# Two attention layers: reciprocal sums applied in the output projection, a ninth P tile, and maxima turned by VectorE

## The chip, the cores and the metric

The kernel runs on one core of a Trainium2 chip. TensorE (PE) multiplies, ACT evaluates exponentials and copies, VectorE (DVE) reduces and does arithmetic between tiles, GpSimd (POOL) adds tiles and issues some DMAs, SyncE (SP) issues most DMAs. Each engine runs its own queue of instructions in order and waits on semaphores for the others. The metric is the device time of one execution in microseconds; lower is better.

## The reference

Two layers of the same kind follow each other. Each is attention over 2048 tokens of width 1024 with 32 heads of width 32, then a routed feed-forward block for the eight best tokens:

```
h   = layernorm(x)
q, k, v = split(h @ wqkv)                  # 32 heads of 32
p   = softmax(q k^T * 32**-0.5)            # 2048 x 2048 per head
x   = x + (p v) @ wo                       # output projection
h   = layernorm(x);  r = h @ w_r           # router score per token
top = 8 tokens with the largest r
y   = (silu(h[top] @ w_gate) * (h[top] @ w_up)) @ w_down
x   = x + h;  x[top] += y * sigmoid(r[top])   # residual of the layernormed rows
```

What matters here: softmax needs the maximum of each row before the exponential, and the sum of the exponentials after it. The kernel multiplies unnormalised exponentials with v and divides by the sum later.

## The kernel before

A layer has three stages: layernorm and the projection to q, k, v; attention; the output projection with the router. The feed-forward block of layer 0 runs beside the start of layer 1.

**Attention** is cut into 32 units per layer. A unit is a group of four heads (g, eight of them) and a quarter of the queries (qc, 512 of them). A unit has 16 steps, one for each 128 keys; step s belongs to unit u = s // 16 and key tile kt = s % 16. In a step TensorE computes the scores of four heads (`scores`, L457), ACT exponentiates them into a tile P (128 × 2048, L767), and TensorE multiplies the P tile of the step before with v (`pv_step`, L685). Besides, TensorE computes plain scores 22 steps ahead (`pre_mm`, L442), and VectorE reduces them to negated maxima (L450), for a later unit. When a unit's maxima are complete, `nm_combine` (L463) takes the minimum over four parts, and `nm_row` (L466 to L475) turns the 128 × 16 result: TensorE transposes it, ACT copies it, SP stores it to DRAM and loads it into one row of the q tile, where it takes part in the product of the scores.

The sum of the exponentials of a unit runs over its 16 P tiles. `MERGED` (L34) names pairs of tiles that a DMA of GpSimd's queue adds in place (`merge`, L700). `ADDED` (L35) names the additions into an accumulator on GpSimd (`acc_add`, L697) as pairs (step, tile). `DIRECT` (L36) names tiles that TensorE sums itself. At step 20 (`SUM_AT`), `sum_mm` (L707) multiplies the direct tiles and the accumulator with ones, four groups in all. `sum_out` copies the result (L714) and stores it, `sum_load` loads it narrow, `recip` inverts it (L724) and stores it, `r_load` loads it broadcast over 32 rows per head, and `norm` lets GpSimd multiply the unit's result with it (L737) and stores the product to `oT` in DRAM. `unit_events` gives the step, the place within the step and the order of each of these. There are eight buffers for P (`PB`); a tile's buffer comes free when its product with v and its merge, addition or sum are done. In the last unit of a layer VectorE does the additions (twelve), and its sum stays in PSUM: VectorE inverts and applies it (L831, L832) after the first weights of the next stage are ready.

**The output projection** (L842 to L878) takes 16 tiles of 128 tokens. `load_o(t)` loads all heads of a tile of tokens from `oT` into `oraw` (two buffers), `split_o(t)` makes two parts of it for the product: ACT rounds (L813), VectorE takes the remainder (L814). The products with `woh` and `wol`, the two parts of the weights, follow (L848, L849, L852). In the loop for tile t VectorE adds the residual (L854), then `split_o(t + 2)`, then the layernorm's statistics (L118, L120), GpSimd works on the statistics (L122 to L862), and SP stores them (`mrd`). After that SP's queue has `load_o(t + 4)`, the load of the residual of tile t + 2, the store of tile t and one load of feed-forward weights.

All orders are those of the program text: each engine executes its instructions in the order in which the loops issue them, and tiles wait for their buffers.

## Time and profile before

| What | Value |
|---|---|
| time, median of 3 runs | 4825.82 us (4814.48 to 4838.82) |
| time of the profiled execution | 4831.82 us |
| its span, first to last instruction | 4829.9 us |
| mean granted TensorE clock | 0.981 |
| busy: PE, DVE, POOL, ACT | 97%, 66%, 63%, 50% |
| exponentials of layer 0, first to last | 613.0 to 2133.6 us |
| exponentials of layer 1, first to last | 3002.5 to 4528.4 us |

A row of a group gives line, engine, operation, output and inputs, the count, the busy time and the mean of one in ns, then the idle time of the engine before these instructions and what ended it. A row of a timeline gives the start and length in us, engine, line, operation, and in brackets the idle time before it with what ended it. SPq are DMAs issued by SP; their length is that of the issue, not of the transfer. A row of stretches gives the stretch, its length, and the busy time of PE, PEld (weight loads), DVE, ACT and POOL, then the granted clock, the share of the DMA engines and GB/s.

### The profile page before, as it was taken

Reading aid. Unit: us, or ns where it says so; the run is one execution under the profiler, and the core shown is the slowest. Engines: PE = TensorE matmul, PEld = TensorE weight load, DVE = VectorE, ACT = ScalarE, POOL = GpSimd, SP = SyncE. Lnnn points to the kernel's source line nnn. Section 1 sums busy time; section 2 is a strip of 40 time slices with the busy share of each in tenths; the row PEclk is TensorE's granted clock in tenths of the full one; section 3 lists DMA queues with packets and bytes.
Section 4 is the critical chain, followed back from the end, with each engine's and each line's share of the span. In section 5 each row is a group of like instructions: output and inputs, shape, how many; then the busy total and the mean of one; then the engine's idle time right before and its main releaser. Section 6 shows DMA issues by size and latency. Waiting matters only on the chain.

```text
span 4829.9 us, 75205 instructions
## 1 busy us (share of the span) xinstructions
PE 4662.7 (97%) x30014; PEld 2737.4 (57%) x30014; DVE 3177.4 (66%) x4919; ACT 2437.1 (50%) x2612; POOL 3023.1 (63%) x1249
## 2 busy tenths in 40 slices
PE   8999999999999999999799999999999999999996
PEld 6887654544445544448577777445444454454572
DVE  3221478888888888875522225888888888888653
ACT  2222266666666666651122222666666666666400
POOL 4443367787778787854433332777777777787551
PEclk9999999999999999999999999999999999999997
DMA  6656477777777777737679564777767677777488
GB/s 196 184 175 176 140 158 156 170 163 152 172 149 166 164 157 161 174 86 235 211 246 270 182 178 133 161 154 164 164 148 170 152 156 169 157 164 166 106 223 288
DMA packets 360815, 832.61 MB, mean 172 GB/s; under 512 B 55000, under 2 KB 187096, under 8 KB 310528
## 3 DMA queue, kind: packets, MB, share of 16 engines
q1 hardware_dynamic: 313296, 494.18, 34.6%
q0 software_dynamic: 47168, 333.63, 34.3%
q8 instruction: 235, 3.85, 0.3%
q14 instruction: 116, 0.95, 0.1%
HBM read 383.47 MB, written 119.14 MB: 104 GB/s over the span
## 4 chain that ended last, share of the span: by engine, by line
PE 79%; DMA 12%; DVE 2%; issue 2%; POOL 2%; SPq 1%; ACT 1%; POOLq 0%; ACTq 0%; DVEq 0%
PE pv L685 18%; PE pre L457 16%; PE st L442 13%; PE st L553 7%; PE st L555 7%; PE st L554 7%; PE st L707 4%; DMA out_dram<-x,pi 3%; DMA P<-P 2%; POOL acc L697 2%; DMA nmx<-nmr 1%; PE pre L852 1%; PE pre L849 1%; PE pre L848 1%; DMA q<-nmx 1%
## 5 line engine op out<-in xcount | busy, mean ns | idle before, releaser
L450 DVE TENSOR_REDUCE nm<-st 128x1 f32<-128x512 f32 x3920 | 2438.9, 684 | 472.7 <-PE st L442 459.5
L767 ACT ACTIVATE P<-pre 128x1024 f32<-128x1024 f32 x2048 | 1985.2, 1022 | 781.0 <-PE pre L457 573.4
L697 POOL TENSOR_TENSOR acc<-acc,P 128x2048 f32<-128x2048 f32 x372 | 1737.6, 4671 | 58.1 <-DMA P<-P 35.2
L457 PE MATMUL pre<-q,ks 64*128 64x512 f32 (+1 forms) x8192 | 1170.6, 399 | 26.9 <-ACT P L767 15.4
L685 PE MATMUL pv<-P,v 128*32 128x512 f32 x8192 | 1101.7, 610 | 2.6 <-DMA v<-vd 2.6
L442 PEld LDWEIGHTS st<-ks,q 64*128 64x128 f32 x3920 | 553.2, 185 | 882.6 <-DVE nm L450 732.9
L442 PE MATMUL st<-ks,q 64*128 64x512 f32 x3920 | 998.6, 469 | 7.3 <-DVE nm L450 5.8
L457 PEld LDWEIGHTS pre<-q,ks 64*128 64x128 f32 (+1 forms) x8192 | 790.5, 188 | 213.9 <-ACT P L767 75.6
L499 POOL TENSOR_TENSOR wl<-wraw,wh 128x2048 fp32r<-128x2048 f32 (+1 forms) x97 | 441.9, 4556 | 677.4 <-ACT wh L498 664.8
L553 PE MATMUL st<-xh,wh 128*128 128x512 f32 x1536 | 616.7, 401 | 2.2 <-ACT xh L525 2.2
L555 PE MATMUL st<-xl,wh 128*128 128x512 f32 x1536 | 602.0, 392 | 0.6 <-DVE xl L526 0.5
L554 PE MATMUL st<-xh,wl 128*128 128x512 f32 x1536 | 601.0, 391 | 0.0
L700 POOL DMA_DIRECT2D P<-P x310 | 272.0, 887 | 298.5 <-PE st L442 258.7
L697 POOL TENSOR_TENSOR acc<-P 128x2048 f32<-128x2048 f32 x62 | 283.9, 4579 | 259.7 <-DMA P<-P 237.6
L569 DVE TENSOR_TENSOR lo<-st,hi 128x512 fp32r<-128x512 f32 x128 | 88.3, 690 | 433.5 <-ACT hi L568 433.5
L568 ACT CAST hi<-st 128x512 fp32r<-128x512 f32 x128 | 75.3, 588 | 558.6 <-PE st L555 553.2
L553 PEld LDWEIGHTS st<-xh,wh 128*128 128x128 f32 x1536 | 290.0, 189 | 104.3 <-issue 30.5
L555 PEld LDWEIGHTS st<-xl,wh 128*128 128x128 f32 x1536 | 289.8, 189 | 64.6 <-DVE xl L526 1.7
L554 PEld LDWEIGHTS st<-xh,wl 128*128 128x128 f32 x1536 | 290.3, 189 | 56.3
L685 PEld LDWEIGHTS pv<-P,v 128*32 128x32 f32 x8192 | 162.2, 108 | 268.5 <-issue 262.9
L535 DVE COPY vn<-st 128x512 f32<-128x512 f32 x64 | 44.3, 692 | 318.5 <-PE st L533 318.5
L848 PE MATMUL pre<-woh,oh 128*128 128x512 f32 x512 | 201.8, 394 | 11.8 <-DVE woh L827 5.7
(163 smaller groups left out, 2649.4 us busy)
## 6 DMA issues: line engine op xcount, KB each, us to landing
P<-P POOLq DMA_DIRECT2D x310, 1024.0 KB, 8.2
wraw<-in_A_wqkv_dram SPq DMA_DIRECT2D x96, 1024.0 KB
q<-qh SPq DMA_DIRECT2D x256, 128.0 KB
ks<-kh SPq DMA_DIRECT2D x128, 256.0 KB
fw<-in_B_w_down_dram SPq DMA_DIRECT2D x28, 1024.0 KB
qh<-hi SPq DMA_DIRECT2D x64, 256.0 KB
ql<-lo SPq DMA_DIRECT2D x64, 256.0 KB
kh<-hi SPq DMA_DIRECT2D x64, 256.0 KB
```

The costliest lines, as they stand in the source:

```text
L442: pe.matmul(ps[b], Q[u][rows, i, 0, qt * 128:(qt + 1) * 128], KS[(u // QC) % 2][rows, i, 0, j * 512:(j + 1) * 512], start=True, stop=True, ...
L450: dve.tensor_reduce(NM[u][:, j, 2 * i + b:2 * i + b + 1, qt], ps[b], axis=AX.X, op=OP.max, negate=True)
L457: pe.matmul(p[:, b * 512:(b + 1) * 512], KS[(u // QC) % 2][rows, i, slot, kt * 128:(kt + 1) * 128], Q[u][rows, i, slot, :], start=(slot == ...
L499: pool.tensor_tensor(wl[:, :, sl], raw[:, :, sl], wh[:, :, sl].bitcast(F32), op=OP.subtract)
L553: pe.matmul(p, wh[:, a, wsl], xh[:, a, :], start=(a == 0), stop=False)
L554: pe.matmul(p, wl[:, a, wsl], xh[:, a, :], start=False, stop=False)
L555: pe.matmul(p, wh[:, a, wsl], xl[:, a, :], start=False, stop=(a == KD - 1))
L685: pe.matmul(PV[u][32 * h:32 * h + 32, :], V[g][:, kt, 32 * h:32 * h + 32], P[s][:, h, :], start=(kt == 0), stop=(kt == NT - 1), tile_posit ...
L697: (dve if on_dve else pool).tensor_tensor(o, a, P[u * NT + k].rearrange("p h c -> p (h c)"), op=OP.add)
L700: pool.dma_start(P[u * NT + a], P[u * NT + b], accum_op=OP.add)
L767: act.activation(P[s][:, 2 * i:2 * i + 2, :].rearrange("p h c -> p (h c)"), p, AF.Exp, scale=SCALE)
L848: pe.matmul(p[:, bl], oh[:, a, :], woh[:, a, bl], start=(a == 0), stop=False)
```

## The change

Five things are changed together.

1. The unit's product with v is stored to DRAM as it is (`pv_step`); `r_load`, `store_o` and `norm` are gone. The reciprocals stay in DRAM, and in the output projection `load_o` loads them too, with four broadcast loads per tile of tokens into `rden`; `split_o` begins with a product on VectorE.
2. The last unit of a layer takes the same way through DRAM as the others (`sum_out`, `sum_load`, `recip` right after its last step), in place of L830 to L833.
3. P has nine buffers; other tiles are merged and added, eight additions on GpSimd instead of seven; two direct tiles instead of three, so `sum_mm` has three groups. In the last unit VectorE adds thirteen tiles.
4. The maxima are turned by a VectorE transpose of 32 × 32 blocks in `nm_row`, one step after `nm_combine`, and stored with four DMAs; TensorE's transpose and ACT's copy are gone.
5. For room, `oraw` and `rden` have one buffer each (`oraw` had two), `o` two instead of three, `sm` one instead of two; the loads of tiles are issued as `load_o(t + 3)`, and before the loop only three tiles are loaded, with `split_o(0)` ahead of `load_o(1)`.

```diff
-PB = 8
-MERGED = (0, 2, 5, 8, 10)
-ADDED = ((6, 4), (8, 2), (9, 7), (11, 5), (13, 8), (15, 12), (17, 10))
-DIRECT = (13, 14, 15)
-SUM_AT = 20
+PB = 9
+MERGED = (2, 4, 6, 8, 11)
+ADDED = ((5, 1), (7, 2), (8, 4), (12, 6), (13, 8), (14, 10), (17, 11), (19, 13))
+DIRECT = (14, 15)
+SUM_AT = 21
...
-    ev += [(SUM_AT, "mid", 5, "sum", ()), (22, "end", 5, "sumload", ()), (24, "mid", 5, "recip", ()),
-           (25, "end", 5, "rload", ()), (27, "end", 5, "norm", ())]
-    return ev
+    return ev + [(SUM_AT, "mid", 5, "sum", ()), (23, "end", 5, "sumload", ()), (25, "end", 5, "recip", ())]
...
+    NMC = []
+    for i in range(2):
+        NMC.append(cons.tile([128, 32], F32R, name=f"nmc{i}"))
+        pool.memset(NMC[i].bitcast(F32), 0.0)
...
         def nm_combine(u):
-            c = small.tile([128, 16], F32, name="nmc")
-            dve.tensor_reduce(c, NM[u].rearrange("p j h t -> p (h t) j"), axis=AX.X, op=OP.min)
-            NMC[u] = c
+            dve.tensor_reduce(NMC[u % 2][:, 0:16], NM.pop(u).rearrange("p j h t -> p (h t) j"), axis=AX.X, op=OP.min)
         def nm_row(u):
-            p = ps_st()
-            pe.transpose(p[0:16, 0:128], NMC.pop(u), ident)
-            t = small.tile([16, 128], F32R, name="nmr")
-            act.copy(t, p[0:16, 0:128])
-            dma(nmx[u], t)
+            t = small.tile([128, 32], F32R, name="nmr")
+            dve.transpose(t.bitcast(F32), NMC[u % 2].bitcast(F32))
+            for b in range(4):
+                dma(nmx[u][:, 32 * b:32 * b + 32], t[32 * b:32 * b + 16, :])
...
-                    act.copy(o, PV[u])
-                    PV[u] = o
+                    act.copy(o, PV.pop(u))
+                    dma(oT[g, :, u % QC * 512:(u % QC + 1) * 512], o)
...
-                for v in list(NMC):
-                    nm_row(v)
                 emit(s, "mid")
                 if pr and pr[1] == 15:
                     nm_combine(pr[0])
+                if pr and pr[1] == 0 and pr[0] > 1:
+                    nm_row(pr[0] - 1)
+                if s + LEAD == NS:
+                    nm_row(NU - 1)
                 emit(s, "end")
                 if s == NS + 1:
-                    last_sum = sum_mm(NU - 1)
+                    sum_out(NU - 1)
+                    sum_load(NU - 1)
+                    recip(NU - 1)
...
             def load_o(t):
-                OR[t] = wp.tile([128, NG, 128], F32, name="oraw")
+                OR[t] = wp.tile([128, NG, 128], F32, name="oraw", bufs=1)
                 dma(OR[t], oT[:, :, t * 128:(t + 1) * 128].rearrange("g p c -> p g c"))
+                RD[t] = wp.tile([128, NG, 128], F32, name="rden", bufs=1)
+                qc, i = divmod(t, 4)
+                for h in range(4):
+                    part = rd.rearrange("(g q) h c -> h q g c", q=QC)[h, qc, :, i * 128:(i + 1) * 128]
+                    dma(RD[t][32 * h:32 * h + 32], part[None].to_broadcast([32, NG, 128]))
             def split_o(t):
                 raw = OR.pop(t)
+                dve.tensor_tensor(raw, raw, RD.pop(t), op=OP.mult)
...
             load_o(0)
             load_x(0)
+            split_o(0)
             load_o(1)
             load_x(1)
-            split_o(0)
...
-            rl = wop.tile([128, 512], F32, name="rl", bufs=1)
-            dve.reciprocal(rl, last_sum)
-            dve.tensor_tensor(rl, PV[NU - 1], rl, op=OP.mult)
-            dma(oT[NG - 1, :, (QC - 1) * 512:QC * 512], rl)
             split_o(1)
             load_o(2)
-            load_o(3)
...
-                if t + 4 < NT:
-                    load_o(t + 4)
+                if t + 3 < NT:
+                    load_o(t + 3)
```

22 lines of the change are left out of this document (5 added, 17 removed).

## The prediction

> **What bounds the kernel now.** I read the page first, there the chain that ended last, by engine.
>
> ```profile
> PE 79%; DMA 12%; DVE 2%; issue 2%; POOL 2%; SPq 1%; ACT 1%; POOLq 0%; ACTq 0%; DVEq 0%
> ```
>
> TensorE carries 79% of it, DMA 12%. So a microsecond that leaves TensorE's stream is worth a microsecond, and any new hole in that stream costs its full length. Next I read the groups that the change touches, by line and shape.
>
> ```profile
> L767 ACT ACTIVATE P<-pre 128x1024 f32<-128x1024 f32 x2048 | 1985.2, 1022 | 781.0 <-PE pre L457 573.4 <-ACT P L767 144.7 <-DMA P<-P 33.2
> L697 POOL TENSOR_TENSOR acc<-acc,P 128x2048 f32<-128x2048 f32 x372 | 1737.6, 4671 | 58.1 <-DMA P<-P 35.2 <-ACT P L767 8.0 <-PE pre L457 1.1
> ...
> L697 POOL TENSOR_TENSOR acc<-P 128x2048 f32<-128x2048 f32 x62 | 283.9, 4579 | 259.7 <-DMA P<-P 237.6 <-ACT P L767 11.3 <-DVE nm L450 5.5
> L700 POOL DMA_DIRECT2D P<-P x310 | 272.0, 887 | 298.5 <-PE st L442 258.7 <-issue 27.3 <-PE pv L685 4.4
> ```
>
> The reader is to see GpSimd's load per unit of attention (a unit is 16 steps; there are 32 per layer): in 62 of the 64 units seven additions of about 4.67 us (372 + 62 of them over both shapes), five merge issues of 0.89 us and one product with the reciprocals (L737, a row of it further down). The exponentials lost only 33.2 us to late merges. Then the timeline, TensorE's and VectorE's rows: each row is the first product of a step, of the step with the sum and of two ordinary ones, and VectorE's four reductions of one step.
>
> ```profile
> 1241.58 0.50 PE L442 MATMUL st<-ks,q 64*128 64x512 f32 x2
> ...
> 1247.71 0.50 PE L442 MATMUL st<-ks,q 64*128 64x512 f32 x2
> ...
> 1250.41 0.50 PE L442 MATMUL st<-ks,q 64*128 64x512 f32 x2
> ```
>
> ```profile
> 1250.95 2.48 DVE L450 TENSOR_REDUCE nm<-st 128x1 f32<-128x512 f32 x4 [0.22 <-PE st L442]
> ```
>
> An ordinary step lasts from 1247.71 to 1250.41: 2.70 us. The step with the sum runs from 1241.58 to 1247.71: 6.13 us, so the sum costs 3.43 us in four groups of 0.86 us. VectorE works 2.48 us of 2.70 and idles 0.22 per step; it is nearly as full as TensorE. The transpose of the maxima, a group of its own:
>
> ```profile
> L468 PE MATMUL st<-ident,nmc 128*16 128x128 f32 x64 | 17.7, 277 | 0.0
> ```
>
> With it a unit is 15 × 2.70 + 6.13 + 0.28 = 46.9 us.
>
> **The change in attention.**
>
> *Three sum groups.* One group of 0.86 us leaves TensorE per unit: 64 × 0.86 = 55 us gained. Nothing else fills that place, because the step around it is limited by TensorE.
>
> *Maxima turned by VectorE.* TensorE's transpose and ACT's copy go: 62 × 0.28 = 17 us. VectorE gets a 128×32 transpose that no row shows. Bounds: nothing, if it fits in the 0.22 us of idle time, or the whole of two ordinary reductions (2 × 0.62 = 1.2 us per unit, 77 us) if it is as slow as those. I take 0.25 us, the size of its small neighbours in the same place, and since reciprocal, combination and transpose now fall in two neighbouring steps I let 0.06 us per unit reach TensorE: 4 us. Net 13 us. The four narrow stores instead of one, on SP, replace the four loads of reciprocals that stood just ahead of them in SP's queue (the 1.71 us of them are in a fence below), so I cost them at nothing; the cover is the half unit between this place and the first use of the row, and without it 3 × 0.35 us per unit, 65 us, would be the price.
>
> *Nine tiles, eight additions.* GpSimd per unit becomes 8 × 4.67 + 5 × 0.89 = 41.8 us, in a unit of 46.9 − 0.86 − 0.21 = 45.8 us. It fits, with 4 us to spare. I walked the order through with a merge landing 8.2 us after its issue: each tile comes free at least 5 us before the exponential that reuses it; before the change the closest is about 1 us (tile 1, freed when merge 0 lands, three steps after its issue). So late merges should stop costing: between 0 and, with restarts at a lower granted clock, about 60 us; I take 25, somewhat less than the 33.2 us above.
>
> *The product with the reciprocals* leaves GpSimd together with 248 loads, and the unit's result is stored at once. Nothing on the path.
>
> Sum for attention: 55 + 13 + 25 = 93 us gained.
>
> **The change at the border to the output projection.** The rows are the write and read hops of one sum, then the border in layer 0:
>
> ```profile
> 2109.60 1.11 SPq L73 DMA_DIRECT2D sd<-sm  x4
> 2111.73 0.34 SPq L73 DMA_DIRECT2D sc<-sd  x1
> 2119.04 0.34 SPq L73 DMA_DIRECT2D rd<-sc  x1
> 2121.27 1.71 SPq L73 DMA_DIRECT2D rb<-rd  x4
> ...
> 2134.91 0.38 SPq L73 DMA_DIRECT2D oraw<-oT  x1
> ...
> 2139.32 1.04 ACT L813 CAST oh<-oraw 128x1024 fp32r<-128x1024 f32 x1 [3.81 <-DMA oraw<-oT]
> ```
>
> ```profile
> 2124.67 2.52 POOL L737 TENSOR_TENSOR o<-o,rb 128x512 f32<-128x512 f32 x1 [17.55 <-DMA rb<-rd]
> ```
>
> ```profile
> 2137.25 1.04 PE L707 MATMUL st<-acc,ones 128*32 128x512 f32 x8
> 2141.36 0.50 PE L848 MATMUL pre<-woh,oh 128*128 128x512 f32 x1 [3.08 <-ACT woh L827]
> ```
>
> ```profile
> 4531.97 1.04 PE L707 MATMUL st<-acc,ones 128*32 128x512 f32 x8
> 4532.94 0.50 PE L848 MATMUL pre<-woh,oh 128*128 128x512 f32 x1
> ```
>
> Before, the load of the first tile of the projection was issued at 2134.91, while TensorE still worked on the last sum, and the first product started 3.1 us after that sum (2138.3 to 2141.36; in layer 1, 0.2 us after). Now the last unit goes through DRAM as the others do, and SP's queue is in order: four stores of the sum, its load, the store of the reciprocals, and only then the load of tile 0 with its four loads of reciprocals; VectorE's queue likewise holds the first product behind that reciprocal. Step by step from the end of the sum: copy 0.7, store and landing 2.1 (2109.60 to 2111.73), load 0.3 + 1.9 (2121.27 to 2124.67 is 3.4 with 1.7 of issue), reciprocal 0.3, store 0.4: 5.7 us until the load of tile 0 is issued. It lands 4.4 us later (2134.91 to 2139.32), the reciprocals about 1.7 after it, product 1.2, ACT's rounding 1.05, copy of the weights 1.04, waits between them 0.4: 15.5 us. That is 12.4 us more in layer 0 and 15.3 in layer 1. VectorE around the border, its last additions and the inversion of the last sum:
>
> ```profile
> 2118.96 15.17 DVE L697 TENSOR_TENSOR acc<-acc,P 128x2048 f32<-128x2048 f32 x6
> ...
> 2157.26 3.35 DVE L831 RECIPROCAL rl<-st 128x512 f32<-128x512 f32 x1
> ```
>
> The last unit gets a thirteenth addition on VectorE, 15.17 / 6 = 2.5 us; the sum has one group less to do meanwhile (0.86 us) and had to wait for nothing, so the end of the sum moves by 0 to 1.7 us; I take 0, since nine tiles let the exponentials of that unit start earlier. Given back: VectorE no longer inverts the last sum in full (3.35 us and a product of half size), less the new product and a wait on ACT (2.3): about 1.5 us per layer. Together 28 − 3 = 25 us lost.
>
> **The change in the output projection.** Each of its 16 tiles per layer takes TensorE 10.9 us. One of them, VectorE's rows and SP's; the two rows of L854 follow the ends of two tiles' products, 10.9 us apart:
>
> ```profile
> 2249.67 1.23 DVE L854 TENSOR_TENSOR x<-pre,x 128x1024 f32<-128x1024 f32 x1 [4.01 <-PE pre L852]
> 2250.81 1.22 DVE L814 TENSOR_TENSOR ol<-oraw,oh 128x1024 fp32r<-128x1024 f32 x1
> 2251.94 1.28 DVE L118 BATCH_NORM_STATS2 bst<-x 128x6 f32<-128x512 f32 x2
> ...
> 2260.55 1.23 DVE L854 TENSOR_TENSOR x<-pre,x 128x1024 f32<-128x1024 f32 x1 [4.01 <-PE pre L852]
> ```
>
> ```profile
> 2256.55 0.32 SPq L73 DMA_DIRECT2D mrd<-mr  x1
> 2256.92 0.42 SPq L73 DMA_DIRECT2D oraw<-oT  x1
> ```
>
> Today tile t+2's data are there before they are needed, since two raw buffers are loaded two tiles ahead. After the change there is one raw buffer and one for the reciprocals, so the load of tile t+3 can only be issued after the split of t+2; and in SP's queue it stands behind the store of tile t's statistics, which VectorE computes only after that split. VectorE waits in order for the load. This closes a ring: load landed, product 1.2, ACT's rounding 1.05 (now behind the product, not early), remainder 1.2 with 0.1 of handover, then as in the rows 2251.94 to 2256.92 the statistics, GpSimd's chain and the store's issue, 5.0 us: 8.5 us from landing to the next load's issue. The ring's period is 8.5 us plus the landing of 1 MB: 512 KB of raw tile and 512 KB of reciprocals in four loads. Today the raw tile is off this ring.
>
> How long that landing takes no row shows. From below: 4.4 us, the idle-chip value of the raw tile above, with the reciprocals keeping up. From above: 10.6 us, a scattered 512 KB in the same stage:
>
> ```profile
> out_dram<-x,pi POOLq DMA_INDIRECT x16, 10.6
> ```
>
> The nearest are the 2-us stretches after the load issued at 2256.92 (the last columns are the granted clock, the DMA share and GB/s):
>
> ```profile
> 2258.00:2260.00 2.00, 2.00 (x11) 1.65 (x10) 0.00 (x0) 0.00 (x0) 0.86 (x1) 1.00 0.34 101
> 2260.00:2262.00 2.00, 2.00 (x11) 1.65 (x10) 1.45 (x2) 1.05 (x1) 0.00 (x0) 1.00 0.17 44
> 2262.00:2264.00 2.00, 2.00 (x11) 1.65 (x10) 2.00 (x3) 0.00 (x0) 0.00 (x0) 1.00 0.80 272
> ```
>
> 101, 44 and 272 GB/s are 0.83 MB up to 2264, so the 0.5 MB of the raw tile arrive some 6.5 us after issue, with the DMA engines two thirds idle. I add 1.5 us for the reciprocals behind it: 8.0 us, a period of 16.5. Ends: 12.9 and 19.1. Thirteen periods per layer (loads 3 to 15) at 16.5 − 10.9 (10.9 in layer 0, about 11.2 in layer 1): 73 + 69 = 142 us lost. At the ends 49 and 209.
>
> On this landing the Trainium skill ("DMA: Bandwidth & Descriptors", the section on the anatomy of one DMA) has a rule: about 2.0 us fixed plus the bytes at 436 GB/s. For 1 MB that is an estimated 4.4 us. The trace disagrees in this stage: half the bytes needed 6.5 us at 2256.92. By the rule the ring would be 12.9 us and the total would come out as in the first rival.
>
> **Sum.** −93 + 25 + 142 = +74 us on the profiled execution (span 4829.9 us, time 4831.82): 4906. That execution lies 6 us above the median of 4825.82, so I predict 4900 for the median.
>
> **Rivals.**
> *The loads land quickly* (the other side). Landing in 4.4 us, period 12.9, loss 49: −93 + 25 + 49 = −19, 4807. It decides where 26 × (period − 11.05) equals 68 us, a period of 13.7 or a landing of 5.2 us. For it: the idle value of 4.4, and a longer period leaves the DMA queues emptier. Against it: the slow stretches above had empty engines too. Faster if the late merges also give more than 25. Chance 0.17.
> *The ring is slower still.* Landing 10.6 us, period 19.1: −93 + 25 + 209 = +141, 4967. For it: the scattered store, and nine DMAs per tile instead of five. Chance 0.15.
> *GpSimd becomes attention's bound.* If waits for merges bring its 41.8 us to 48 per unit, 62 × 2.2 = 136 us come on top: 5036. For it: additions right after a merge take longer, and they waited for merges. Against: the 4 us to spare. It decides once those waits exceed 4 us per unit. Chance 0.08.
>
> **How the numbers follow.** The forecast (landing 6 to 9.5 us, 4850 to 4945) has 0.60. About 0.5% (24 us) is what a measurement of this kernel tells from no change. Of the first rival I give 0.10 to faster and 0.07 to the same; of the forecast's lower edge 0.05 to the same; the rest is slower: 0.10, 0.12, 0.78. The range, 4810 to 4985, leaves out 0.1 on each side: the quick landing with all stalls recovered below, GpSimd and the worst ring above.
>
> **What the profile after would show.** The sum step at 5.3 us instead of 6.13, no L468, eight GpSimd additions per unit, and fewer waits of the exponentials on merges. In the projection the additions that end each tile (L854 before) spaced 15 to 18 us instead of 10.9, TensorE waiting for the remainder (ol), VectorE's new product waiting for DMA, a lower granted clock there, and some 15 us between the last sum and the first product. I am wrong if the tiles stay below 13 us, which would say that the loads land in about 4 us, or if units grow beyond 46 us.

## The result, and the profile after

The changed kernel takes 5126.8 us (median of four executions, 5112.2 to 5133.8) against 4832.3 us for the kernel before beside it (four, 4814.5 to 4841.6): a ratio of 1.061, 95% interval 1.0568 to 1.0653. The prediction was 4900 us, with 4810 to 4985 as its range: slower, as forecast, but by four times as much. The profiled execution has a span of 5119.0 us, 289 more than before. From the starts of the first and the ends of the last exponentials (L767 before, L752 after), the first product of the output projection and the last addition that ends a tile:

| Stage | before | after | difference | predicted |
|---|---|---|---|---|
| start of layer 0, to its first exponential | 613.0 | 623.5 | +10.5 | 0 |
| attention, layer 0 | 1520.6 | 1538.8 | +18.2 | together −93 |
| attention, layer 1 | 1525.9 | 1514.2 | −11.7 | |
| border to the projection, layer 0 | 7.8 | 20.7 | +12.9 | together +25 |
| border, layer 1 | 4.6 | 19.7 | +15.1 | |
| output projection, layer 0 | 185.7 | 309.0 | +123.3 | together +142 |
| output projection, layer 1 | 190.1 | 310.4 | +120.3 | |
| the rest | 782.3 | 782.7 | +0.4 | 0 |

The page of the changed kernel first: the chain that ended last, by engine, and the groups of exponentials and of the projection's first products.

```profile
PE 71%; DMA 15%; DVE 4%; SPq 3%; POOL 3%; issue 3%; ACT 1%; DVEq 0%; POOLq 0%; ACTq 0%
...
L752 ACT ACTIVATE P<-pre 128x1024 f32<-128x1024 f32 x2048 | 1985.7, 1022 | 845.5 <-PE pre L459 640.8
...
L838 PE MATMUL pre<-woh,oh 128*128 128x512 f32 x512 | 242.3, 473 | 219.9 <-DVE pre L856 184.7
```

TensorE's share of the chain falls from 79% to 71%; DMA, SP and VectorE take most of it. The exponentials no longer list a wait for merges (33.2 us before), yet idle more, 845.5 us against 781.0. The projection's products wait 219.9 us; 184.7 of them for L856, the router's product on VectorE, which stands in VectorE's queue behind the waiting split, and not for the remainder as forecast.

**The output projection.** VectorE's rows and SP's for two tiles of layer 0:

```profile
2318.52 1.22 DVE L844 TENSOR_TENSOR x<-pre,x 128x1024 f32<-128x1024 f32 x1
2328.70 1.23 DVE L805 TENSOR_TENSOR oraw<-oraw,rden 128x1024 f32<-128x1024 f32 x1 [8.96 <-DMA rden<-rd]
2331.12 1.23 DVE L809 TENSOR_TENSOR ol<-oraw,oh 128x1024 fp32r<-128x1024 f32 x1 [1.19 <-ACT oh L808]
...
2336.72 1.22 DVE L844 TENSOR_TENSOR x<-pre,x 128x1024 f32<-128x1024 f32 x1
```

```profile
2319.09 0.38 SPq L71 DMA_DIRECT2D oraw<-oT  x1
2319.58 2.00 SPq L71 DMA_DIRECT2D rden<-rd  x4
...
2336.87 0.32 SPq L71 DMA_DIRECT2D mrd<-mr  x1
2337.29 0.38 SPq L71 DMA_DIRECT2D oraw<-oT  x1
```

This is the ring of the prediction. The load issued at 2319.09 is there when the product starts, 2328.70, after 9.61 us; from there to the next load's issue (2337.29) it is 8.59 us. Over the 24 inner tiles of both layers (3 to 14) the landing, from the first issue to the product, has a median of 11.3 us (9.6 to 12.8), and the tiles are on average 19.8 us apart in layer 0 and 20.0 in layer 1. Over the whole stage of layer 0, first in the kernel before, then in the changed one, the granted clock (the column after the five busy times) and TensorE's busy time (the third number) are:

```profile
2141.40:2327.00 185.60, 178.80 (x776) 145.30 (x776) 109.75 (x132) 18.79 (x19) 87.99 (x109) 0.99 0.59 186
```

```profile
2183.00:2492.00 309.00, 213.56 (x776) 167.43 (x776) 122.98 (x145) 18.89 (x19) 87.61 (x109) 0.82 0.52 138
```

TensorE was busy for 178.8 of 185.6 us; now it is for 213.6 of 309.0, at a clock of 0.82, and even its busy time is longer.

**The border.** Its length is about the one worked out, but not its steps:

```profile
2166.83 1.12 SPq L71 DMA_DIRECT2D sd<-sm  x4
2168.97 0.34 SPq L71 DMA_DIRECT2D sc<-sd  x1
2171.04 0.34 SPq L71 DMA_DIRECT2D rd<-sc  x1
2171.48 0.37 SPq L71 DMA_DIRECT2D oraw<-oT  x1
```

```profile
2170.76 0.25 DVE L723 RECIPROCAL sc<-sc 128x16 f32<-128x16 f32 x1 [7.48 <-DMA sc<-sd]
2179.68 1.22 DVE L805 TENSOR_TENSOR oraw<-oraw,rden 128x1024 f32<-128x1024 f32 x1 [8.67 <-DMA rden<-rd]
```

Tile 0 with its reciprocals lands 8.2 us after the issue at 2171.48 (7.2 us in layer 1), where 4.4 + 1.7 = 6.1 were taken.

**Attention.** It was to gain 93 us and lost 6. I took the time of each of the 16 steps from the starts of the exponentials. The sum of the steps' medians is an undisturbed unit; the mean over units 0 to 29 of a layer holds the stalls too:

| us per unit | undisturbed | mean, layer 0 | mean, layer 1 |
|---|---|---|---|
| before | 46.9 | 47.9 | 48.1 |
| after | 45.9 | 48.4 | 47.5 |

The undisturbed unit shrank by 1.0 us. But there is a new stall at step 10 of a unit: in about a third of the units this step takes 4 to 9 us, mostly 7 to 9, instead of 2.8. One of them, on VectorE, SP, GpSimd and TensorE:

```profile
796.75 0.27 DVE L464 TENSOR_REDUCE nmc<-nm 128x16 fp32r<-128x64 f32 x1
799.38 0.25 DVE L723 RECIPROCAL sc<-sc 128x16 f32<-128x16 f32 x1 [2.36 <-DMA sc<-sd]
799.55 2.41 DVE L452 TENSOR_REDUCE nm<-st 128x1 f32<-128x512 f32 x4
```

```profile
792.43 0.34 SPq L71 DMA_DIRECT2D sc<-sd  x1
```

```profile
791.65 0.88 POOL L699 DMA_DIRECT2D P<-P  x1
```

```profile
800.24 0.79 PE L444 MATMUL st<-ks,q 64*128 64x512 f32 x1 [2.16 <-DVE nm L452]
800.96 1.93 PE L684 MATMUL pv<-P,v 128*32 128x512 f32 x8
```

The reciprocal stands in VectorE's queue and waits for the 8 KB of sums. Their load was issued at 792.43, 0.8 us after a merge of 1 MB, and landed 6.95 us later; at the border, with no merge about, the same load took 1.79 us (2168.97 to 2170.76). The trace says the same over all units: where this load was issued 0.5 to 2.3 us after a merge, VectorE waited 1.4 to 4.4 us for it in 19 of 20 units; where it was issued sooner or later than that, at most 0.2 us (the last unit of each layer aside). Behind the reciprocal queue the step's reductions, TensorE runs out of score buffers, and then works at half speed (1.93 us for eight products that take 1.06 otherwise; the granted clock is 0.51 from 800 to 803 us). Step 10 is longer than its median by 1.85 us on average in layer 0 and 1.22 in layer 1: 30 × 3.07 = 92 us. The rest of what attention lost are stalls of about 0.4 us per unit at step 15 and the last two units of each layer, 3.9 and 5.3 us longer than before. The Trainium skill ("DMA: Bandwidth & Descriptors", the section on issuing engines not being separate DMA queues) says that DMAs issued by different engines run on the same DMA engines and interleave; the 6.95 us against 1.79 fit that.

### The profile page after: what moved, and what is told of

Read it like the earlier page. It is cut to its first block, busy times and chain, and to the rows that moved or that the text cites. A ratio compares the mean times of both kernels' runs of the same rounds, so it can differ in the third digit from the quotient of the medians.

```text
span 5119.0 us, 74160 instructions
## 1 busy us (share of the span) xinstructions
PE 4693.8 (92%) x29438; PEld 2761.8 (54%) x29438; DVE 3215.5 (63%) x5015; ACT 2422.8 (47%) x2550; POOL 3230.2 (63%) x1251
## 4 chain that ended last, share of the span: by engine, by line
PE 71%; DMA 15%; DVE 4%; SPq 3%; POOL 3%; issue 3%; ACT 1%; DVEq 0%; POOLq 0%; ACTq 0%
PE pv L684 17%; PE pre L459 15%; PE st L444 12%; PE st L552 7%; PE st L554 7%; PE st L553 7%; DMA rden<-rd 5%; PE st L706 3%; SPq L71 3%; DMA sc<-sd 2%; DMA sd<-sm 2%; DMA q<-nmx 1%; DMA nmx<-nmr 1%; DMA q<-ql 1%; POOL acc L696 1%
## 5 line engine op out<-in xcount | busy, mean ns | idle before, releaser
L752 ACT ACTIVATE P<-pre 128x1024 f32<-128x1024 f32 x2048 | 1985.7, 1022 | 845.5 <-PE pre L459 640.8
L696 POOL TENSOR_TENSOR acc<-acc,P 128x2048 f32<-128x2048 f32 x434 | 2012.9, 4638 | 271.7 <-DMA P<-P 255.8
L838 PE MATMUL pre<-woh,oh 128*128 128x512 f32 x512 | 242.3, 473 | 219.9 <-DVE pre L856 184.7
L699 POOL DMA_DIRECT2D P<-P x310 | 293.2, 946 | 225.0 <-PE st L444 216.0
L124 POOL TENSOR_TENSOR rs<-mv,eps_c 128x1 f32<-128x1 f32 x64 | 13.8, 216 | 476.6 <-DVE mv L122 476.6
L808 ACT CAST oh<-oraw 128x1024 fp32r<-128x1024 f32 x32 | 33.5, 1047 | 568.3 <-DVE oraw L805 549.5
```

What stands on the lines that cost most here:

```text
L696: (dve if on_dve else pool).tensor_tensor(o, a, P[u * NT + k].rearrange("p h c -> p (h c)"), op=OP.add)
L699: pool.dma_start(P[u * NT + a], P[u * NT + b], accum_op=OP.add)
L752: act.activation(P[s][:, 2 * i:2 * i + 2, :].rearrange("p h c -> p (h c)"), p, AF.Exp, scale=SCALE)
L838: pe.matmul(p[:, bl], oh[:, a, :], woh[:, a, bl], start=(a == 0), stop=False)
```

## The experiments

The kernel before ran again beside each group of runs, with medians from 4832 to 4842 us; a difference of less than about 10 us between kernels of different groups is therefore not read as one.

**The reciprocal two steps later.**

```diff
-    return ev + [(SUM_AT, "mid", 5, "sum", ()), (23, "end", 5, "sumload", ()), (25, "end", 5, "recip", ())]
+    return ev + [(SUM_AT, "mid", 5, "sum", ()), (23, "end", 5, "sumload", ()), (27, "end", 5, "recip", ())]
```

> The changed kernel with one edit: the reciprocal of a unit's sums is put two steps later in VectorE's queue (after step 11 of the next unit instead of after step 9). Theory A (VectorE stalls at the reciprocal because the load of the sums, issued right behind a 1 MB merge, lands some 7 us after its issue, and the next step's reductions queue behind it): the waits of the reciprocal for the load (58 us in the profile of the changed kernel) go, step 10 of each unit falls back to the 2.70 us of the others, and the two attention stages get about 90 us shorter; I take 80 since a late load can still be met: 5127 - 80 = 5047. Rival B (the stall is that of the merges or of the P tiles, and the reciprocal only shows it): step 10 stays long or another step takes it over, 5110 to 5130. The output projection stays at about 19.8 us per tile in either case.

Measured: 5041.6 us, 85 less. Attention is 1490.3 and 1483.2 us, 48.5 and 31.0 less than in the changed kernel; all else is as it was. So the stall was the reciprocal's place. What is left is 0.5 to 0.6 us per unit at step 9 and 0.1 to 0.2 at step 10, and one of these stalls shows its cause, in the rows of SP and of TensorE of this kernel:

```profile
1015.37 0.80 SPq L71 DMA_DIRECT2D q<-qh  x2
```

```profile
1024.94 0.76 PE L444 MATMUL st<-ks,q 64*128 64x512 f32 x1 [2.10 <-DMA q<-qh]
```

The first scores ahead of a later unit wait for its q rows, whose loads SP issues one per step, now around the stores of the sum.

**The projection's loads ahead of the statistics' store.**

```diff
+                if t + 3 < NT:
+                    load_o(t + 3)
                 dma(mrd[t * 128:(t + 1) * 128, :], mr)
...
-                if t + 3 < NT:
-                    load_o(t + 3)
```

> The changed kernel with one edit in the output projection: the load of tile t+3 is issued ahead of the store of tile t's statistics in SP's queue, no longer behind it. Theory A (a ring of landing plus 8.6 us from landing to the next issue, of which about 5 us are statistics, GpSimd's chain and that store): the part of 8.6 us shrinks to the product, the rounding and the remainder, 1.2 + 1.05 + 1.3 + handover = 3.7 us; with a landing of 11.2 us the period goes from 19.8 to about 14.9 us, 26 periods x 4.9 = 127 us less: 5000. Rival B (the loads themselves, or other DMA work in the stage, set the period): the landing grows by what the issue is earlier, the period stays above 18 us, over 5080.

Measured: 4917.5 us, 209 less; the projection takes 208.8 and 218.3 us, its tiles are 12.4 and 12.9 apart. From product to next issue it is 3.67 us, as expected. Of the 209 us, 192 lie in the two projections. The landing fell too, to a median of 8.6 and 9.0 us (6.7 to 12.7); that was expected by neither theory, and the next runs show where it comes from. Two tiles:

```profile
2299.86 1.22 DVE L805 TENSOR_TENSOR oraw<-oraw,rden 128x1024 f32<-128x1024 f32 x1 [3.06 <-DMA rden<-rd]
...
2313.38 1.23 DVE L805 TENSOR_TENSOR oraw<-oraw,rden 128x1024 f32<-128x1024 f32 x1 [4.28 <-DMA rden<-rd]
```

```profile
2303.53 0.37 SPq L71 DMA_DIRECT2D oraw<-oT  x1
```

The ring is the reason for the long stage, and two lines moved within SP's queue take 192 of its 244 us away.

**What the landing is made of.** Four kernels change only what is loaded; they leave out or replace the reciprocals, so their outputs are not the reference's. One loads the reciprocals once:

```diff
-                RD[t] = wp.tile([128, NG, 128], F32, name="rden", bufs=1)
+                if t:
+                    return
+                RD[0] = wp.tile([128, NG, 128], F32, name="rden", bufs=1)
...
-                dve.tensor_tensor(raw, raw, RD.pop(t), op=OP.mult)
+                dve.tensor_tensor(raw, raw, RD[0], op=OP.mult)
```

> The changed kernel, but the tile of reciprocals is loaded once, for the first tile of the output projection, and every product uses it; the four loads of reciprocals of the other 15 tiles are left out, so the output is not that of the reference. Theory A (the reciprocals' four loads are what makes the landing long): the landing falls from 11.2 to the 6.5 us that I read for a raw tile alone in the profile before, the period from 19.8 to 15.1, 26 x 4.7 = 122 us less: 5005. Rival B (the raw tile itself lands that late and the reciprocals come alongside): the period stays within 1.5 us of 19.8, over 5085. By the Trainium skill (DMA: Bandwidth & Descriptors, anatomy of one DMA), 512 KB would take an estimated 3.2 us and the period would be 11.8, 26 x 8.0 = 208 us less: 4919.

Measured: 5025.6 us, 101 less; periods of 15.9 and 16.0 us, landings of 7.3 and 7.4. A raw tile alone takes 7.3 us; I had read 6.5. The four loads of reciprocals add 4.0. In the next, they read 32 different rows each:

```diff
-                    part = rd.rearrange("(g q) h c -> h q g c", q=QC)[h, qc, :, i * 128:(i + 1) * 128]
-                    dma(RD[t][32 * h:32 * h + 32], part[None].to_broadcast([32, NG, 128]))
+                    part = oT[:, 32 * h:32 * h + 32, t * 128:(t + 1) * 128].rearrange("g p c -> p g c")
+                    dma(RD[t][32 * h:32 * h + 32], part)
```

> The changed kernel, but the tile of reciprocals is filled from rows of the raw output (32 different rows per load instead of one row read 32 times), in as many loads of the same size, so the output is not that of the reference. Theory A (the loads are long by their number of 512-byte pieces): landing and period as in the changed kernel, 19.8 us within 1, 5105 to 5150. Rival B (32 reads of one DRAM row wait for each other): the landing falls by 2 to 4 us, the period to 16 to 18 us, 5030 to 5080.

Measured: 5134.3 us, landings of 11.2 and 11.5 us. Reading one row 32 times costs nothing extra that could be seen. Next, pieces of 4 KB instead of 512 bytes for both tiles:

```diff
-                dma(OR[t], oT[:, :, t * 128:(t + 1) * 128].rearrange("g p c -> p g c"))
+                dma(OR[t], src[t * 128:(t + 1) * 128, :].rearrange("p (g c) -> p g c", g=NG))
...
-                    part = rd.rearrange("(g q) h c -> h q g c", q=QC)[h, qc, :, i * 128:(i + 1) * 128]
-                    dma(RD[t][32 * h:32 * h + 32], part[None].to_broadcast([32, NG, 128]))
+                    part = src[t * 128 + 32 * h:t * 128 + 32 * h + 32, :].rearrange("p (g c) -> p g c", g=NG)
+                    dma(RD[t][32 * h:32 * h + 32], part)
```

> The changed kernel, but raw tile and reciprocals of the output projection are filled with rows of the layer's input, each partition's 4 KB in one piece instead of eight of 512 bytes, in as many loads of the same size and place, so the output is not that of the reference. Theory A (the number of pieces makes the landing long): it falls from 11.3 us to 4.5 to 6 us (by the Trainium skill, DMA: Bandwidth & Descriptors, anatomy of one DMA, an estimated 4.4 us), the period from 19.8 to 13 to 14.6 us, 5127 - 26 x 5.2 to 6.8 = 4950 to 4990. Rival B (five DMAs, their issue and the other transfers of the stage set it): landing above 9 us, period above 17.5, over 5065.

Measured: 5076.4 us, periods of 17.8 and 18.7; the landing is 9.2 us in layer 0 and 9.9 in layer 1. The number of pieces is 1.5 to 2 us of the 11.3, not most of it. Last, the same with one load of the second tile instead of four (the edit against the run just shown):

```diff
-                for h in range(4):
-                    part = src[t * 128 + 32 * h:t * 128 + 32 * h + 32, :].rearrange("p (g c) -> p g c", g=NG)
-                    dma(RD[t][32 * h:32 * h + 32], part)
+                dma(RD[t], src[t * 128:(t + 1) * 128, :].rearrange("p (g c) -> p g c", g=NG))
```

> The kernel with rows of the input in 4 KB pieces (landing 9.3 us in layer 0), and the reciprocals' tile filled by one load instead of four, so two DMAs per tile instead of five; the output is not that of the reference. Theory A (each of the five DMAs costs its issue of some 0.5 us on SP ahead of the last one's data): landing falls by 1.5 us to 7.8, period from 17.8 to 16.3. Rival B (the landing is set by the bytes and by the transfers of the same stage): within 0.5 us of 9.3, period 17.3 to 18.

Measured: 5033.7 us, periods of 16.2 and 16.4, landings of 7.7 us: the three loads saved are worth 1.6 us in layer 0 and 2.0 in layer 1. The first tile of the same kernel, and one in the stage:

```profile
2191.10 0.37 SPq L71 DMA_DIRECT2D oraw<-in_A_x_dram  x1
2191.70 0.33 SPq L71 DMA_DIRECT2D rden<-in_A_x_dram  x1
...
2313.92 0.43 SPq L71 DMA_DIRECT2D oraw<-in_A_x_dram  x1
2314.45 0.39 SPq L71 DMA_DIRECT2D rden<-in_A_x_dram  x1
```

```profile
2195.85 1.23 DVE L803 TENSOR_TENSOR oraw<-oraw,rden 128x1024 f32<-128x1024 f32 x1 [5.22 <-DMA rden<-in_A_x_dram]
...
2321.44 1.23 DVE L803 TENSOR_TENSOR oraw<-oraw,rden 128x1024 f32<-128x1024 f32 x1 [6.88 <-DMA rden<-in_A_x_dram]
```

1 MB in two loads of long pieces lands 4.75 us after the issue at 2191.10, but 7.5 us after that at 2313.92. So of 11.3 us in layer 0 some 4.8 are the bare transfer, 2.9 come with the stage, 1.6 with three more loads and 2.0 with short pieces. What makes the 2.9 can be read from the rate (last column) between 1.0 and 3.5 us after the issue, for the same two tiles and then for tile 0 and the tile of 2319.09 of the changed kernel:

```profile
2192.10:2194.60 2.50, 0.00 (x0) 0.00 (x0) 0.00 (x0) 0.00 (x0) 0.00 (x0) 0.50 0.95 331
2314.92:2317.42 2.50, 2.50 (x8) 1.94 (x7) 0.00 (x0) 0.00 (x0) 0.87 (x1) 0.56 1.10 33
```

```profile
2172.48:2174.98 2.50, 0.00 (x0) 0.00 (x0) 0.00 (x0) 0.00 (x0) 0.00 (x0) 0.50 0.91 251
2320.09:2322.59 2.50, 2.50 (x7) 1.91 (x7) 0.00 (x0) 0.00 (x0) 0.88 (x1) 0.53 0.35 92
```

The load in the stage starts slowly, at 33 and 92 GB/s. In the changed kernel this holds for all 26 loads that SP issues right behind a store of statistics (78 to 109 GB/s), and for none of the six others (249 to 261). That store has 128 pieces of 8 bytes. The residual's load follows in every case, and no weights are loaded near tile 3, which starts slowly too. In the run with the load ahead of the store no load starts below 170 GB/s, and the landing was 2.3 to 2.7 us shorter. So the store of statistics just ahead is the likeliest cause of the 2.9 us. GpSimd's addition to x starts at the same moment, ends some 2 us before the rate recovers, and no run takes the two apart. The Trainium skill ("DMA: Bandwidth & Descriptors", anatomy of one DMA) gives, for a DMA that GpSimd issues, 2.0 us plus the bytes at 436 GB/s, an estimated 4.4 us for 1 MB. These loads are SP's; the 4.75 us, 0.6 of it up to the second issue, come near that, and the 11.3 do not.

**Two buffers.** The feed-forward weights give up a prefetch buffer in each layer (4 + 5 and 10 instead of 5 + 5 and 11).

```diff
-                OR[t] = wp.tile([128, NG, 128], F32, name="oraw", bufs=1)
+                OR[t] = wp.tile([128, NG, 128], F32, name="oraw", bufs=2)
...
-                RD[t] = wp.tile([128, NG, 128], F32, name="rden", bufs=1)
+                RD[t] = wp.tile([128, NG, 128], F32, name="rden", bufs=2)
...
+            load_o(3)
...
-                if t + 3 < NT:
-                    load_o(t + 3)
+                if t + 4 < NT:
+                    load_o(t + 4)
```

> The changed kernel with two raw tiles and two tiles of reciprocals in the output projection, loaded two tiles ahead as before the change (load of t+4 at the end of tile t); the 4 KB for each come from one prefetch buffer less for the feed-forward weights. Theory A (the one buffer closes the ring and the ring alone makes the stage long): a load issued at the end of tile t is needed some 20 us later, its landing of 11 us is hidden, the tiles come back to 10.9 to 11.3 us, the two stages get 230 us shorter: 4895. Rival B (the DMA engines or SP's queue cannot bring 1 MB per 11 us beside the rest): the period stays at 13 us or more, above 4940. The border (+28 us) and attention's stall stay.

Measured: 4903.5 us, 223 less; the projection takes 190.7 and 199.5 us, periods of 11.3 and 11.9. The ring alone made the stage long. It keeps 0.4 to 0.7 us per tile over the kernel before. The room has a price: what the table above calls the rest is 787 to 791 us in this and the four later kernels with two buffers, 4 to 8 more than in the changed kernel.

**Which part of attention does what.** Eight tiles and the old order, with the rest of the change kept:

```diff
-PB = 9
+PB = 8
-MERGED = (2, 4, 6, 8, 11)
+MERGED = (0, 2, 5, 8, 10)
-ADDED = ((5, 1), (7, 2), (8, 4), (12, 6), (13, 8), (14, 10), (17, 11), (19, 13))
+ADDED = ((6, 4), (8, 2), (9, 7), (11, 5), (13, 8), (15, 12), (17, 10))
-DIRECT = (14, 15)
+DIRECT = (13, 14, 15)
```

> The changed kernel with the order of P tiles, merges, additions and sum of the kernel before (eight tiles, seven additions, four sum groups, the sum at step 20, its load after step 22, the reciprocal after 24); the products in the output projection and the maxima by VectorE stay. Theory A (the new order gains 93 - 13 = 80 us when nothing stalls and loses it again in the stall at step 10): attention as before less 13 us, so about 20 us faster than the changed kernel, 5107. Rival B (the stall belongs to the four stores of maxima or to VectorE's extra work): the stall is here too, attention gets 80 to 100 us longer than before, 5190 to 5210.

Measured: 5041.8 us, 85 less than the changed kernel: neither theory. Attention is 1481.6 and 1481.2 us, 39 and 45 less than in the kernel before, which has the same order of tiles. The undisturbed unit is 46.63 us and the mean is 46.64 and 46.63: no stall is left in sixty units. So the ninth tile is not needed for that. What held up the kernel before has to be something that this kernel leaves out; GpSimd's waits in the kernel before, which the prediction did not read, show a candidate (in us, times, longest):

```profile
POOL acc L697 <- DMA P<-P: 272.7, 86, 7.6
POOL o L737 <- DMA rb<-rd: 101.3, 53, 17.5
```

The first wait is no sign of trouble: it comes to 280.2 us with eight tiles, where nothing stalls. The second is: GpSimd stood at the product with the reciprocals, waiting for their load, with merges and additions queued behind it. Two of these waits, 35 us together, come before the last product of each layer, when GpSimd has nothing else to do; the others are 66 us. In all eight units with a wait above 2.5 us, the sixteen steps after it lost 1.0 to 8.5 us; of fifty units with a shorter one, eleven lost a microsecond or more. So what ends the late merges is that the product and its loads are gone. That GpSimd's wait is how they did the harm fits these rows; no run takes the product away and leaves the loads.

The other part alone, in the kernel before: the maxima turned by VectorE (the hunks of `nm_combine` and `nm_row`).

> The kernel before with one part of the change: the maxima are turned by VectorE and stored in four pieces, in the two steps of the change. The prediction's term: 17 us of TensorE saved, 4 us given back, so 13 us faster, 4819 against 4832. Rival (VectorE is too full for it): the transposes' 62 x 0.2 us and their place cost what they save, 4832 to 4850. If the first q, k and v projection is 10 us longer here too, the two constant tiles for the maxima are the reason (all tiles behind them lie 256 bytes further).

Measured: 4864.5 us against 4841.5, a ratio of 1.0046 (1.0025 to 1.0067): slower. The start of layer 0 is 11 us longer, attention 6 and 15 us. The stalls of the kernel before are still here, 0.8 and 1.1 us per unit. Step 10 falls from 3.12 to 2.76 us, but step 15 grows from 2.74 to 3.50 and 3.56, because the first scores of a unit wait for its row of maxima; TensorE's waits in this kernel, of the weight loads and of the products, add up to 72.6 us where the kernel before has 22.3:

```profile
PEld pre L461 <- DMA q<-nmx: 43.0, 42, 2.7
PE pre L461 <- DMA q<-nmx: 29.6, 34, 2.3
```

Here the four loads of reciprocals still stand ahead of the four stores in SP's queue. In the run with eight tiles, where they are gone, the same waits come to 0.3 us; in the changed kernel, with nine tiles, to 35.1.

**The three repairs together.** Two buffers, the late reciprocal, and the last sum behind the first tile's loads:

```diff
-                    sum_out(NU - 1)
-                    sum_load(NU - 1)
-                    recip(NU - 1)
+                    last_sum = sum_mm(NU - 1)
...
             load_o(1)
...
+            sm = wp.tile([128, D], F32, name="xn", bufs=1)[:, 0:512]
+            act.copy(sm, last_sum)
+            for h in range(4):
+                dma(sd[NU - 1, h:h + 1, :], sm[32 * h:32 * h + 1, :])
             split_o(1)
+            sum_load(NU - 1)
             load_o(2)
+            load_o(3)
+            recip(NU - 1)
```

> The changed kernel with three edits: two buffers as in the run before, the reciprocal two steps later, and the last unit's sum stored, loaded and inverted behind the loads and the split of the first tile of the output projection instead of ahead of them (tile 0 needs no reciprocal of the last unit). Theory A (ring, stall and border are separate and add up): 5127 - 230 - 80 - 25 = 4792, 0.8% below the kernel before. Rival B (the border's time only moves, or the stall does): 4830 to 4870. The 10 us by which the first q, k and v projection is longer than before should stay.

Measured: 4800.7 us, a ratio of 0.9903 (0.987 to 0.9936) to the kernel before: faster than both kernels. Attention and projection came back as expected. The border gave 5 us per layer and not 12: it is 15.7 and 15.1 us, since the load of tile 0, issued before the last sum is done, still takes 10.1 and 8.7 us to land and the product and the rounding follow it.

**Loads of q earlier.** One more edit to that kernel:

```diff
-                if loads:
+                for _ in range(2 if kt in (3, 4) else 1):
+                    if loads:
```

> The kernel with all three edits (4801), and one more: of the loads that a unit issues one per step from step 2 on, two are issued in steps 3 and 4 each, so the q rows of the unit after next are on their way before the sum's stores hold SP's queue. Theory A (what is left of stalls at steps 9 and 10, some 0.6 us per unit, is the reduction products' wait for those q rows): steps 9 and 10 fall to 2.70, both attention stages together get 35 to 45 us shorter, 4760. Rival B (two loads in a step delay the merges or the loads of maxima, or the waits move to step 15): 4790 to 4810.

Measured: 4821.9 us (0.9966, 0.9956 to 0.9976), 21 more and above both theories. Steps 9 and 10 did fall to 2.65 and 2.70 us. But now the sum at step 5 waits for GpSimd's accumulator; TensorE's waits in this kernel (in the kernel with three repairs the first row has 14.1 us, in 7 cases):

```profile
PEld st L706 <- POOL acc L696: 66.2, 37, 5.1
PE st L706 <- POOL acc L696: 36.3, 28, 4.2
```

The rows of maxima come later as well: TensorE's waits for them go from 10.6 to 37.7 us. With nine tiles GpSimd has little room: eight additions and five merges are 42 us of a unit of 46, and what TensorE gains ahead it loses at the sum and at step 15. Why the sum's accumulator is later here was not tried.

**Eight tiles with the repairs.** The old order of tiles again, two buffers and the border mended.

> The kernel with two buffers and the border mended, but with the order of the kernel before for P tiles, additions and sum (eight tiles, seven additions, four sum groups, reciprocal after step 24). Theory A (the stalls of the kernel before came from GpSimd's product waiting for its reciprocals, and with it gone eight tiles are enough): units of 46.6 us without stalls, attention 1481 us per layer as in the run with eight tiles, so within 10 us of the kernel with all three edits, 4790 to 4800. Rival B (nine tiles pay): 4830 or more.

Measured: 4798.9 us, 0.9931 (0.9912 to 0.9949), which cannot be told from the 4800.7 with nine tiles. Attention takes 1487.0 and 1480.2 us, against 1488.2 and 1480.4 with nine tiles, the late reciprocal and a sum group less. The undisturbed unit of nine tiles is 0.83 us shorter (45.80 against 46.63), but 0.9 and 0.6 us of stalls per unit and two last units that together take 5 to 6 us longer per layer use it up.

**The start of layer 0.** Its code is the same in all kernels. First the two constant tiles alone, in the kernel before:

```diff
+    NMC = []
+    for i in range(2):
+        NMC.append(cons.tile([128, 32], F32R, name=f"nmc{i}"))
+        pool.memset(NMC[i].bitcast(F32), 0.0)
```

> The kernel before with nothing but the two constant tiles of 128x32 that the change allocates and fills (256 bytes per partition; nothing reads them). Theory A (every tile allocated behind them lies 256 bytes further, and that alone slows the products of layer 0's q, k and v projection, 11 us in each kernel that has the tiles): the first exponential starts at about 624 us instead of 613, everything else as before, 4850. Rival B (the 11 us come from what else the change does): the first exponential at 613, 4840. The kernel before ran at 4841 beside the last runs.

Measured: 4838.5 us (ratio 1.0002), first exponential at 613.0 us: the constants, and with them a shift of the other tiles by 256 bytes, are not it. In the change the maxima's small tiles shrink as well, and what counts is where the tiles behind them end up:

```diff
+    pool.memset(cons.tile([128, 32], F32, name="pad"), 0.0)
```

> The changed kernel with one more constant tile of 128x32 (128 bytes per partition, nothing reads it). In the build of the kernel before, the tile that holds the transposed input (xh) starts at byte 224 of a 256-byte block; with the constants alone added it also did, and the stage took as long as before; in the changed kernel and in the one with the transposes alone it starts at byte 96, and the stage is 11 us longer. With this tile it starts at 224 again. Theory A (where the operands of the products start decides): first exponential at 613 us, whole kernel about 11 us faster, 5116. Rival B (something else in these kernels): 624 as in the changed kernel.

Measured: the first exponential at 612.8 us, 10.7 earlier. The whole came to 5122.7 us, only 4 less; in the profiled execution attention's stalls were longer. One group of products between 130 and 230 us, in the changed kernel and, one line further down, in this one:

```profile
L552 PE MATMUL st<-xh,wh 128*128 128x512 f32 x135 | 54.1, 401 | 0.0
```

```profile
L553 PE MATMUL st<-xh,wh 128*128 128x512 f32 x139 | 55.0, 396 | 0.0
```

In 100 us 139 of these products are done instead of 135, at a mean of 396 ns instead of 401. All tiles behind the constants, `xh` among them, start 128 bytes further, and nothing else differs.

**Everything that the runs point to.** Eight tiles, two buffers, the border mended, and the 128 bytes.

> The kernel with two buffers, the border mended and the order with eight tiles (4799), with the tile of 128 bytes of the run before. If theory A of that run holds: 11 us less, 4788, 1.0% below the kernel before. If not: 4799.

Measured: 4789.2 us, 0.9899 (0.9879 to 0.9919), the lowest median of all; as a ratio to the kernel before beside it, it cannot be told from the three repairs together (0.9903). Its stages are 613.2 us to the first exponential, 1482.8 and 1481.5 us of attention, borders of 14.7 and 15.3, projections of 190.7 and 196.6.

## Why the prediction was right or wrong

The sign was right and the mechanism that carried it, the ring, was there. The size was wrong: +289 us instead of +74 on the profiled execution. Of the 215 us between them 102 lie in the output projection, 100 in attention, 10.5 at the start of layer 0 and 3 at the borders. Two steps failed: the term for the landing, 8.0 us where 11.3 were measured, and in attention a new wait of 92 us, that of the moved reciprocal, for which the sum had no term.

*The output projection, +142; measured +244.* The part from landing to the next issue was right, 8.5 us against 8.6. The term that was mis-sized is the landing, 8.0 against 11.3, beyond the upper end of 10.6. I took 6.5 us for the raw tile, by when its bytes had passed, where the run with the reciprocals loaded once shows 7.3; and I added 1.5 us for the reciprocals "behind it", where they cost 4.0, through more DMAs and short pieces. The two stretches at 101 and 44 GB/s that I read as the pace of the transfer lie right behind a store of statistics (2256.55), as the slow starts of the changed kernel do. The longer landing is 26 × 3.3 = 86 us; the other 16 are the first and the last interval of each layer, 2.5 to 5.8 us longer than before, which the thirteen periods left out. The upper end was the wrong row too: one scattered store of 512 KB does not bound five loads of 1 MB together.

*Three sum groups and the maxima, −68; measured about −60.* The undisturbed unit fell from 46.9 to 45.9 us, where 45.8 was predicted.

*The four narrow stores at nothing, in place of the loads of reciprocals; 65 us without cover.* Nearly right, and both sides were seen: without the loads of reciprocals the waits for the row of maxima come to 0.3 us (eight tiles), with them (the transposes alone) step 15 grows by 0.8 us in 62 units, about 50 us. But the cover is not half a unit: the row is turned at step 10 and first used at step 15.

*Late merges, −25, put down to nine tiles.* The means of the kernel before are 1.0 and 1.2 us above its undisturbed unit, 67 us in sixty units, and with eight tiles and the product gone all of it goes; so more was to be gained, and not by the ninth tile. The prediction's "The product with the reciprocals leaves GpSimd ... Nothing on the path" had that wrong: the product and its loads were what the 67 us hung on. I had read the exponentials' waits for merges and not asked what made the merges late.

*What the prediction left out: the reciprocal's new place.* Event and load move by a step, the load now follows a merge, and VectorE, nearly as full as TensorE, stands still for it. It costs 92 us by the steps, and 85 came back when it was moved. With the undisturbed unit's −60, stalls of 124 us instead of 67, and 9 us more in the last units, attention comes to the +6 that were measured. The rival that a wait takes the place of the one removed was only thought of for GpSimd.

*GpSimd as attention's bound.* Not in the changed kernel, but its 4 us of room are few: with the loads of q earlier the sum waited for its accumulator.

*The border, +28 − 3; measured +28.* Near by luck: the landing of tile 0 took 8.2 and 7.2 us instead of 6.1, the same term as in the ring; the steps around it and the sum, one group shorter, took less than forecast, and what should have been given back did not show.

*The start of layer 0, 0; measured +10.5.* Nothing in the profile before could tell it; the 128-byte run shows where it comes from.

"Slower" came true with the ring that was to carry it; that it came so clearly is owed to the longer landing and to a gain of 93 us in attention that did not come. The range was too narrow because it held the uncertainty of one landing, with a bound from a lone transfer, and no term for a new wait in attention.

## What to carry to other kernels

When a load closes a ring, the ring's order in the issuing queue counts as much as its buffers: moving the loads ahead of one small store gave back 192 of 244 us without a byte of memory, since they no longer waited for that store's turn and no longer started slowly behind it. When tiles come late, look for the instruction in the slow engine's queue that waits for something unrelated, before adding buffers: taking one product and its loads away ended stalls that the ninth tile was meant to end. And where a small load feeds an engine that has no idle time, give it room for landing behind a large transfer, 7 us here and not 2.

## What the runs showed of the hardware that was not expected

- The 8 KB load landed after 1.8 us at the border and after 6 to 9 us when it was issued 0.5 to 2.3 us behind a 1 MB merge.
- 1 MB in five loads of 512-byte pieces landed 11.3 us after the first issue; in two loads of 4 KB pieces it took 7.7 us in the same stage and 4.75 us for the first tile. One row read 32 times was no slower than 32 rows.
- Right behind a store of 128 pieces of 8 bytes, loads moved 78 to 109 GB/s between 1.0 and 3.5 us after their issue, elsewhere in the same stage 249 to 261 (26 and 6 loads of the changed kernel).
- Tiles that start 128 bytes further in SBUF brought the first exponential of layer 0 from 623.5 back to 612.8 us. Why is open; from the last tile of layer 0 to the first exponential of layer 1 it is 675.4 us in the kernel before and 675.8 in the changed one.
- The VectorE transpose of 128 × 32 took 0.20 us (L469 in the trace of the changed kernel).
